# Attention with a local window and global keys, then a SoLU layer: other token runs, sums spread by TensorE in the first batch, constant matmuls and a new order

## The chip, the core and the metric

The kernel runs on one core of a Trainium2 chip. The core has five engines, each with its own row of instructions that it takes strictly in order: TensorE (PE; its weight loads are listed as PEld), VectorE (DVE), ScalarE (ACT), GpSimd (POOL) and SyncE (SP). Transfers between DRAM and the on-chip memory (SBUF) are issued by SP, ACT or POOL and run on 16 DMA engines that all of them share. TensorE writes into PSUM, eight banks of 128 partitions by 2 KB; DVE and ACT read it there. The metric is the device time of one execution in microseconds; less is better.

## What is computed

Four batches, eight heads, 768 tokens, 64 columns a head. A query sees the 8 first keys of its sequence (global) and the 96 keys up to itself (local), with a bias that falls linearly with distance, by a slope for each head. The result, heads side by side, is the 3072 x 512 input x of a feed-forward layer.

```python
scores = scale * np.matmul(q, k.transpose(0, 1, 3, 2))
keep = is_global | is_local
scores = np.where(keep, scores - slopes[:, None, None] * dist, -1e9)
a = np.exp(scores - max); a = a / sum(a)
x = np.matmul(a, v)                       # to 3072 x 512
h = x @ w_in                              # 512 x 1024
solu = h * softmax(h)
ln = (solu - mean) / sqrt(var + 1e-6) * g_ln
out = ln @ w_out                          # 1024 x 512
```

## The kernel before, in words

Everything is written as *steps*: an engine, an estimated duration, a priority, the steps it depends on, the buffers it takes and frees, and a function that emits its instructions. `Plan.order` plays the steps through with these estimates, at each free engine the waiting step of the lowest priority number first, and the functions are then called in that order. The order is therefore fixed before the run: the priorities come from the table `PRIO`, one number for each step, and on the chip each engine waits at the head of its row until that instruction's operands are there. A late operand holds up everything behind it on that engine.

Heads go in pairs: head 2p on partitions 0 to 63, head 2p+1 on 64 to 127. For each batch:

- *Loads.* k and q of a pair come with `load_heads`, eight tokens of 64 columns a head on one partition (`JW` = 8), so 96 partitions hold the 768 tokens and each piece of a transfer has 2,048 bytes. In batch 0 the first 256 tokens come apart in natural order (`load_first`, tiles `knat`, `qnat`), the other 512 in runs of eight on 64 partitions. v comes in blocks of 128 tokens (`load_v`), its first and last 64 tokens for the odd heads with `load_ends` (tile `vt`), the eight global rows with `load_globals` (tile `vgn`).
- *Cast and transposition.* POOL casts to 16 bit (L698, L694), TensorE transposes through PSUM (L714), DVE copies to `kT` (L733) and `qT` (L729). `kT` is put back in token order by that copy; `qT` is left as [8, 96], token 8g + j at [j, g], and so all that has queries as columns has them as eight pieces with a stride, up to the product at the end.
- *Scores.* Blocks of 64 keys against the up to 160 queries that can see them. A bias matmul (L822, from the table `bw`) and a score matmul (L840), both in 64 x 64 blocks of the array, fill a pair of banks; ACT takes the exponential to `eb` (L848). The global keys of all heads are scored at once (L883, then `eg`, L894). Batch 0 has three such groups, of 256 queries each, the other batches two.
- *Sums.* A *unit* is 256 queries (batch 0) or 384. TensorE adds up the exponentials of all heads with blocks of ones (L905, L912), ACT takes a logarithm (L920) and the exponential of its negative (L923), which is the reciprocal. SP stores it to DRAM (`rd`, L553) and loads it back to all 64 partitions of each head (`rb`, L559).
- *Products.* For two pairs at a time TensorE multiplies the exponentials by v (L992) and the global ones by `vgz` (L979) in two half-steps, between which DVE reads one element (`tick`, L1002). DVE multiplies by `rb` and puts the tokens back in order: `xT` (L1019).

For each of the 24 tiles of 128 tokens: the wide projection (L1051, eight matmuls of 512 columns), ACT's exponential (L1058), DVE's product with h (`uu`, L1061), ACT's squares (L1065), eight transposes (L1072) copied by DVE to `uT` (L1076), the output projection (L1110, eight matmuls of 512 columns), ACT's scaling to `osb` (L1116) and SP's store. `w_out` is scaled by g on DVE (L625), its mean over rows is taken by eight matmuls (L631) and subtracted (L635); the output projection needs that.

The lines that set the order around the change:

```python
    def release(self, owner, what, deps):
        self.step("Q", 0, 0, deps, None, free=[(owner, what)])
...
    if PRIO:
        for s, pr in zip(plan.steps, PRIO.split()):
            s["prio"] = int(pr)
    for s in plan.order():
        if s["fn"] is not None:
            s["fn"]()
```

## Time and profile before

| | us |
|---|---|
| median of 3 runs | 222.46 |
| lowest and highest | 219.66, 223.21 |
| the profiled execution: its time | 223.18 |
| the profiled execution: its span, first to last instruction | 221.5 |
| busy in that span: PE, DVE, ACT, POOL | 174.9, 112.6, 112.9, 65.0 |

The profile shows one execution. The page divides the span into 40 equal slices and gives for each the busy share of an engine in tenths. Its list of groups puts together the instructions of one line, operation and shape, with their count, busy time and mean duration. The order of time lists instructions with start, duration and, in brackets, how long the engine was idle before and what ended that. Matmuls overlap, so what a row of them costs is read from start to start. All moved 35.23 MB by DMA.

### The profile page before, as it was taken

Reading aid. Unit: us, or ns where it says so; the run is one execution under the profiler, and the core shown is the slowest. Engines: PE = TensorE matmul, PEld = TensorE weight load, DVE = VectorE, ACT = ScalarE, POOL = GpSimd, SP = SyncE. Lnnn points to the kernel's source line nnn. Section 1 sums busy time; section 2 is a strip of 40 time slices with the busy share of each in tenths; the row PEclk is TensorE's granted clock in tenths of the full one; section 3 lists DMA queues with packets and bytes.
Section 4 is the critical chain, followed back from the end, with each engine's and each line's share of the span. In section 5 each row is a group of like instructions: output and inputs, shape, how many; then the busy total and the mean of one; then the engine's idle time right before and its main releaser. Section 6 shows DMA issues by size and latency. Waiting matters only on the chain. (4 is left out here: it accounts for less than half of the span.)

```text
span 221.5 us, 6271 instructions
## 1 busy us (share of the span) xinstructions
PE 174.9 (79%) x2636; PEld 103.2 (47%) x2636; DVE 112.6 (51%) x238; ACT 112.9 (51%) x202; POOL 65.0 (29%) x140
## 2 busy tenths in 40 slices
PE   0036837677988979997879989779997999998890
PEld 0014416555664646564544546455555455434440
DVE  0465367223574554865534656352772368484540
ACT  2003302432682367693455888364785674566752
POOL 7854187430392166433072008300100000000000
PEclk9999995555999999999988999999999999999998
DMA  6999999994299992999995039631603156300222
GB/s 178 252 202 304 189 206 206 235 259 91 66 259 253 291 222 69 238 251 269 248 231 132 18 113 225 146 145 50 145 0 147 22 130 143 142 3 0 95 95 96
DMA packets 47387, 35.23 MB, mean 159 GB/s; under 512 B 32440, under 2 KB 37120, under 8 KB 47360
## 3 DMA queue, kind: packets, MB, share of 16 engines
q1 hardware_dynamic: 44560, 33.24, 61.1%
q0 software_dynamic: 544, 1.05, 2.9%
q10 hardware_dynamic: 2256, 0.56, 1.1%
q8 instruction: 20, 0.33, 0.7%
q14 instruction: 7, 0.06, 0.1%
HBM read 29.50 MB, written 6.39 MB: 162 GB/s over the span
## 5 line engine op out<-in xcount | busy, mean ns | idle before, releaser
L848 ACT ACTIVATE eb<-bank 128x960 f16<-128x960 f32 (+3 forms) x36 | 29.9, 856 | 48.2 <-PE bank L840 47.7
L1051 PE MATMUL bank<-w_in_sb,xT 128*128 128x512 f16 x192 | 47.1, 389 | 0.1
L1110 PE MATMUL bank<-gw_out_sb,uT 128*128 128x512 f16 x192 | 44.8, 379 | 1.0 <-DVE xT L1019 0.4
L1061 DVE SCALAR_TENSOR_TENSOR uu<-ef,bank 128x1024 f16<-128x1024 f16 x24 | 29.2, 1216 | 12.5 <-ACT ef L1058 12.4
L1058 ACT ACTIVATE ef<-bank 128x1024 f16<-128x1024 f32 x24 | 24.5, 1020 | 16.3 <-PE bank L1051 16.2
L1019 DVE TENSOR_TENSOR xT<-bank,rb 128x384 f16<-128x384 f32 (+1 forms) x36 | 25.2, 730 | 10.1 <-PE bank L992 5.0
L1110 PEld LDWEIGHTS <-uT 128*128 128x128 f16 x192 | 17.8, 97 | 21.3 <-DVE uT L1076 1.4
L1051 PEld LDWEIGHTS <-xT 128*128 128x128 f16 x192 | 17.9, 99 | 20.3 <-issue 1.9
L1065 ACT ACTIVATE sq<-uu 128x1024 f16<-128x1024 f16 x24 | 25.2, 1051 | 3.9 <-DVE uu L1061 3.7
L714 PE MATMUL bank<-ident,k 96*128 96x96 f16 (+2 forms) x136 | 10.2, 220 | 19.5 <-POOL k L694 10.9
L733 DVE COPY kT<-bank 128x768 f16<-128x768 f16 (+2 forms) x20 | 15.4, 769 | 19.4 <-PE bank L714 16.8
L992 PE MATMUL bank<-eb,v 64*64 64x160 f16 (+4 forms) x464 | 20.5, 230 | 4.1 <-DVE tick L1002 1.3
L1076 DVE COPY uT<-bank 128x1024 f16<-128x1024 f16 x24 | 16.4, 689 | 14.1 <-PE bank L1072 6.1
L698 POOL CAST k<-k 96x1024 f16<-96x1024 f32 (+1 forms) x16 | 16.5, 1035 | 23.1 <-PE bank L714 11.3
L698 POOL CAST q<-q 96x1024 f16<-96x1024 f32 (+1 forms) x16 | 16.4, 1036 | 19.9 <-PE bank L714 13.3
L1116 ACT ACTIVATE osb<-bank,rstd 128x512 f32<-128x512 f32 x24 | 15.9, 684 | 11.2 <-PE bank L1110 5.3
L714 PEld LDWEIGHTS <-k 96*128 96x128 f16 (+2 forms) x136 | 7.9, 106 | 23.6 <-POOL k L694 11.1
L992 PEld LDWEIGHTS <-v 64*64 64x64 f16 x464 | 11.8, 107 | 12.1 <-issue 8.1
L822 PE MATMUL bank<-bw,identb 64*64 64x160 f16 (+4 forms) x448 | 16.0, 251 | 0.8 <-DVE uu L1061 0.6
L783 POOL CAST v<-v 128x704 f16<-128x704 f32 (+2 forms) x24 | 13.4, 576 | 10.7 <-DMA v<-in_v_dram 10.0
L840 PE MATMUL bank<-qT,kT 64*64 64x160 f16 (+4 forms) x416 | 15.6, 250 | 0.5 <-DVE qT L729 0.5
L1072 PE MATMUL bank<-ident,uu 128*128 128x128 f16 x192 | 14.4, 219 | 1.8 <-DVE uT L1076 0.9
(82 smaller groups left out, 176.3 us busy)
## 6 DMA issues: line engine op xcount, KB each, us to landing
out_dram<-osb SPq DMA_DIRECT2D x24, 256.0 KB
q<-in_q_dram SPq DMA_DIRECT2D x12, 384.0 KB
k<-in_k_dram SPq DMA_DIRECT2D x12, 384.0 KB
rb<-rd SPq DMA_DIRECT2D x12, 384.0 KB
v<-in_v_dram SPq DMA_DIRECT2D x12, 192.0 KB
w_out<-in_moe_w_out_dram SPq DMA_DIRECT2D x4, 512.0 KB
v<-in_v_dram SPq DMA_DIRECT2D x12, 160.0 KB
rb<-rd SPq DMA_DIRECT2D x6, 256.0 KB
```

Of the source, the lines that this page charges most:

```text
L698: nc.gpsimd.tensor_copy(out=o[0:w], in_=a[0:w].rearrange("p h j d -> p j h d"))
L714: nc.tensor.transpose(out=pt[:, j * m : j * m + m], in_=src[0:m, j].rearrange("p h d -> p (h d)"), identity=ident[0:m, 0:m])
L822: nc.tensor.matmul(out=sc[o : o + 64, par, col : col + n * JW], lhsT=identb[r, r], rhs=v3(bw[r, p])[:, :, a : a + n], start=(par, h) not i ...
L848: ex["fn"] = (lambda ex=ex, qk=qk, gw=gw: nc.scalar.activation(out=eb[at(qk, "eb")][:, :, 0:gw], in_=big(qk)[:, :, 0:gw], func=AF.Exp, sca ...
L992: nc.tensor.matmul(out=o_[64 * h : 64 * h + 64, :, gl : gl + m], lhsT=vv[r, v_at(vi, h, c), d0 + d, :], rhs=view(eb[at(e_own[b, gi, d0 + d ...
L1019: nc.vector.tensor_tensor(out=xT[at(xt_own[b], "xT")][:, p, q0:q1].rearrange("p (g j) -> p g j", j=JW), in0=one(av, d)[:, 0:w].rearrange(" ...
L1051: nc.tensor.matmul(out=ph()[:, ts(fh, 512)], lhsT=xT[at(xt_own[b], "xT")][:, j, ts(t % NA, P)], rhs=w_in_sb[:, j, ts(fh, 512)], start=(j = ...
L1058: ex["fn"] = lambda g1=g1, t=t, ph=ph: nc.scalar.activation(out=ef[at(g1, "ef")], in_=ph(), func=AF.Exp, accum_out=s0[:, t : t + 1])
L1061: u["fn"] = lambda u=u, g1=g1, t=t, ph=ph: nc.vector.scalar_tensor_tensor(out=uu[at(u, "uu")], in0=ef[at(g1, "ef")], scalar=USC, in1=ph(), ...
L1065: sqs["fn"] = lambda u=u, t=t: nc.scalar.activation(out=sq, in_=uu[at(u, "uu")], func=AF.Square, accum_out=s2[:, t : t + 1])
L1076: el["fn"] = lambda lt=lt, el=el: nc.vector.tensor_copy(out=uT[at(el, "uT")].rearrange("p c f -> p (c f)"), in_=one(lt).bitcast(FP16))
L1110: nc.tensor.matmul(out=one(g2), lhsT=uT[at(el_x, "uT")][:, c, :], rhs=gw_out_sb[:, c, :], start=(c == 0), stop=(c == NFC - 1))
```

## The change

It does these things at once.

- *Runs of six.* `load_heads` puts six tokens on each of 128 partitions (pieces of 1,536 bytes); batch 0's rest comes in runs of four (1,024 bytes). Casts are 768 and 512 columns wide on 128 partitions, a pair takes six (four) 128 x 128 transposes instead of eight, and DVE's copy puts both `kT` and `qT` in token order. With that all query columns are contiguous everywhere: scores, `eb`, sums, the products with v and `xT`.
- *Global products.* The product with `vgz` is written as one 64 x 64 block for each head instead of 64 x 128 for two.
- *Sums spread by TensorE in batch 0* (`DIRECT`, three units). No sum step, no store and load of `rd` and `rb`: each pair gets its own two half-steps, in which every matmul with v has a twin with ones (`onesv`, `onesz`), so that the sums come out on all 64 partitions of the head in a second bank. ACT takes logarithm and exponential of it for each pair and DVE multiplies.
- *w_out's first scaling* goes from DVE to ACT. `load_ends` becomes two loads for each batch, eight in all. `uT` has seven buffers instead of four.
- *Constant matmuls.* Where the plan sees TensorE idle by over 330 ns between 3 and 60 us of its own time, before that step it issues matmuls of a constant tile `busy16` (128 x 512) into a bank that is free, for 80% of that gap at 216 ns each: 63 in all, 29 of them ahead of the first transpose, 34 at 13 places up to before the second half of batch 0's products.
- *A new order*: other estimates, at most four large loads under way in the plan (`LDQ`), and another table `PRIO`.

```diff
+    WARM = (3000, 60000)
...
+                    spot = min((i for i in range(8) if banks[i] or i in mine),
+                               key=lambda i: bank_at[i], default=None)
+                    if e == "PE" and now < self.WARM[1] and s["dur"] and spot is not None:
+                        idle = now - max(busy[e], bank_at[spot] + 100, self.WARM[0])
+                        if idle > 330:
+                            s["warm"] = (spot, int(idle * 0.8 / 216))
...
     for s in plan.order():
+        spot, count = s["warm"]
+        for _ in range(count):
+            nc.tensor.matmul(out=bank[spot // 2][:, spot % 2, :], lhsT=busy16[:, 0:P],
+                             rhs=busy16, start=True, stop=True)
...
-    def load_heads(src, dst, b, p, lo, hi):
+    def load_heads(src, dst, b, p, lo, run):
         rows = src[b, 2 * p]
-        n = hi - lo
         nc.sync.dma_start(
-            out=dst[0:n].rearrange("g h j d -> g h (j d)"),
-            in_=bass.AP(tensor=rows.tensor, offset=rows.offset + lo * JW * D,
-                        ap=[[JW * D, n], [S * D, 2], [1, JW * D]]))
+            out=dst[:, 0 : 2 * run * D].rearrange("g (h x) -> g h x", h=2),
+            in_=bass.AP(tensor=rows.tensor, offset=rows.offset + lo * D,
+                        ap=[[run * D, P], [S * D, 2], [1, run * D]]))
...
-            wr.append(step("DVE", 484, 16000 + 100 * j, [w_out_st[j // 2], g_st] + bias_st + [far_st], lambda j=j:
-                           nc.vector.tensor_scalar(
-                               out=gw_out_sb[:, j, :], in0=w_out32[:, j, :],
-                               scalar1=g32[:, j : j + 1], scalar2=None, op0=ALU.mult)))
+            wr.append(step("ACT", 640, 16000 + 100 * j,
+                           [w_out_st[j // 2], g_st] + bias_st + [far_st], lambda j=j:
+                           nc.scalar.activation(
+                               out=gw_out_sb[:, j, :], in_=w_out32[:, j, :], func=AF.Copy,
+                               scale=g32[:, j : j + 1])))
...
-                    for j in range(n):
-                        nc.tensor.transpose(out=pt[:, j * m : j * m + m],
-                                            in_=src[0:m, j].rearrange("p h d -> p (h d)"),
-                                            identity=ident[0:m, 0:m])
+                    for j in range(run):
+                        nc.tensor.transpose(out=pt[:, j * P : j * P + P], in_=src[:, j, :],
+                                            identity=ident)
...
+    DIRECT = {(0, 0), (0, 1), (0, 2)}
...
+            for ti_, duo in enumerate([(p, None) for p in range(NPR)] if direct else
+                                      [(p, p + 1) for p in range(0, NPR, 2)]):
...
                             nc.tensor.matmul(
-                                out=o_[64 * h : 64 * h + 64, :, gl : gl + m],
-                                lhsT=vv[r, v_at(vi, h, c), d0 + d, :],
+                                out=o_[64 * h : 64 * h + 64, gl : gl + m],
+                                lhsT=onesv[r, :] if pv is None else vv[r, v_at(vi, h, c), pair, :],
...
+                if direct:
+                    ln = step("ACT", 110 + w, ta + 1000, [aw, table_st], None, take="lns",
+                              free=[(av, 1)])
+                    re = step("ACT", 140 + w, ta + 1500, [ln], None, take="rr",
+                              free=[(ln, "lns")])
```

Of the order three places matter for what follows. Names are tiles with a running number; the line numbers of the changed program are its own.

SP, the loads around the middle of the load stage. Before, the first k and q of batch 1 (96 partitions) stand among batch 0's v, the v ends and the `rb` of batch 0's first unit:

```order
L498 DMA k_0_92<-in_k_dram 96x2x512
L518 DMA vt_81<-in_v_dram 64x16x64
L498 DMA q_1_96<-in_q_dram 96x2x512
L559 DMA rb_143<-rd_141 64x4x256 x2
L511 DMA v_0_104<-in_v_dram 128x4x64
L498 DMA k_1_93<-in_k_dram 96x2x512
L511 DMA v_1_105<-in_v_dram 128x4x64
```

These are its rows 27 to 33; all of `w_out` (rows 1, 5 and 11) has been asked for long before. Now, rows 46 to 50:

```order
L518 DMA k_0_95<-in_k_dram 128x2x384
L518 DMA q_0_98<-in_q_dram 128x2x384
L644 DMA w_out_70<-in_moe_w_out_dram 128x2x512
L518 DMA k_1_96<-in_k_dram 128x2x384
L518 DMA k_2_97<-in_k_dram 128x2x384
```

The k and q loads of batch 1 come behind all of batch 0, and `w_out` has moved from the front to among them, its last part to row 48.

DVE, around the products of a unit of batch 0. Before, the first unit, with one k copy ahead:

```order
L733 COPY kT_113<-bank_160 128x768
L1002 COPY tick<-bank_157 128x1
L1002 COPY tick<-bank_158 128x1
L1019 TENSOR_TENSOR xT_90<-bank_160,rb_143 128x256
L1019 TENSOR_TENSOR xT_90<-bank_158,rb_143 128x256
L1019 TENSOR_TENSOR xT_90<-bank_157,rb_143 128x256
L729 COPY qT_118<-bank_160 128x768
```

Now, the end of the last two units, with the copies of batch 1 (128x768) among the products:

```order
L750 COPY qT_121<-bank_165 128x768
L1028 COPY tick<-bank_163 128x1
L1056 TENSOR_TENSOR xT_93<-bank_164,rr_141 128x256
L1056 TENSOR_TENSOR xT_93<-bank_165,rr_140 128x256
L750 COPY kT_114<-bank_165 128x768
L1056 TENSOR_TENSOR xT_93<-bank_166,rr_140 128x256
L1056 TENSOR_TENSOR xT_93<-bank_166,rr_141 128x256
L663 SCALAR_TENSOR_TENSOR gw_out_sb<-w_out_70,g_72,bank_163 128x512 x5
```

The products take ACT's reciprocals (`rr`) in place of `rb`, a copy of a batch 1 load stands ahead of the last two, and the second scaling of `w_out` has moved behind all of batch 0's products.

ACT, after the first unit's exponentials. Before, one logarithm and one exponential for the unit:

```order
L894 ACTIVATE eg_116<-bank_160,gbias 128x128
L848 ACTIVATE eb_126<-bank_157 128x2x288
L920 ACTIVATE lns_135<-bank_160 128x256
L923 ACTIVATE rr_137<-lns_135 128x256
L848 ACTIVATE eb_127<-bank_157 128x2x320
```

Now, a pair of them for each pair of heads:

```order
L1033 ACTIVATE lns_138<-bank_166 128x256
L1037 ACTIVATE rr_140<-lns_138 128x256
L1033 ACTIVATE lns_139<-bank_164 128x256
L1033 ACTIVATE lns_138<-bank_165 128x256
L1037 ACTIVATE rr_141<-lns_139 128x256
L1033 ACTIVATE lns_139<-bank_163 128x256
```

All score exponentials of batch 0 but four now stand ahead of these. On TensorE (a list that is too long to show) the first two tiles' projections come behind the first unit's products; then, ahead of the third tile, stand the products of units 1 and 2, four transpose sets of batch 1 and the mean over `w_out`, and all scores of batch 1 come behind it. Before, the third tile stood behind the first two tiles' output projections and all scores of batch 1.

More of the change, by code (lines that the diff above doesn't have):

```diff
@@ L21 @@
 WIN = 160
-JW = 8
-BG = BLK // JW
-WG = WIN // JW
+RUN = 6
 USC = 1.0 / 16.0
@@ L686, in do_part, with cast @@
                     need = [dma]
[L687 removed]
+                cs = step("POOL", 394 if natural else 20 + 1.01 * n, t0 - 1200, need, None,
                           take=nm + "16_", free=[(iss, nm + "32_")] if iss else [])
[L690 to L692 removed]
+                def cast(cs=cs, iss=iss, x32=x32, x16=x16, nm=nm, run=run, natural=natural, p=p):
+                    o = x16[at(cs, nm + "16_")][:, 0:run].rearrange("p j (h d) -> p j h d", h=2)
@@ L918 @@
-            sm["fn"] = sums
-            ln = step("ACT", 110 + w, tS + 1000, [sm], None, free=[(sm, "one")])
-            ln["fn"] = lambda sm=sm, w=w: nc.scalar.activation(
-                out=lns[at(sm, "lns")][:, 0:w], in_=one(sm)[:, 0:w], func=AF.Ln)
-            re = step("ACT", 140 + w, tS + 1500, [ln], None, take="rr", free=[(sm, "lns")])
-            re["fn"] = lambda re=re, sm=sm, w=w: nc.scalar.activation(
-                out=rr[at(re, "rr")][:, 0:w], in_=lns[at(sm, "lns")][:, 0:w], func=AF.Exp, scale=-1.0)
@@ L937 @@
[L937 to L946 removed]
+            direct = (b, ui) in DIRECT
@@ new lines @@
+            lastu = ui == len(UNITS[b]) - 1
+            if lastu:
+                plan.release(kg_own[b], "kg", kg_users)
+                for p in range(NPR):
+                    plan.release(own[p, "k"], "kT", qk_of[p])
+                    plan.release(own[p, "q"], "qT", qk_of[p])
+            turn_of = []
+            by = [[x for x in todo if x[2] == par] for par in range(2)]
+            turns = [[(i, d) for i in range(max(map(len, by))) for d in (0, 1)
+                      if i < len(by[ph ^ d])] for ph in range(2)]
@@ new lines, in pe @@
+                        pv = duo[d]
+                        pair = duo[0] if pv is None else pv
+                        o_ = one(av, d)[:, 0:w]
+                        for h in range(2):
+                            x = h ^ par
+                            r = slice(64 * x, 64 * x + 64)
+                            if i < 0:
+                                nc.tensor.matmul(
+                                    out=o_[64 * h : 64 * h + 64, x * n : x * n + n],
+                                    lhsT=(onesz[r, 2 * pair + h] if pv is None else
+                                          vgz[r, b, 2 * pair + h, :]),
+                                    rhs=eg[at(gs, "eg")][r, 0:hw_],
+                                    start=False, stop=False,
+                                    tile_position=(64 * x, 64 * h), skip_group_check=True)
+                                continue
+                            gi, c, _, col, nn, lo, gl, m = by[par][i]
+                            nc.tensor.matmul(
+                                out=o_[64 * h : 64 * h + 64, gl : gl + m],
+                                lhsT=onesv[r, :] if pv is None else vv[r, v_at(vi, h, c), pair, :],
+                                rhs=view(eb[at(e_own[b, gi, pair], "eb")], r, par, col, nn,
@@ L1094, in stats @@
                 nc.vector.tensor_tensor(out=a, in0=a, in1=c, op=ALU.add)
-            st = step("DVE", 850, tt + 5700, [chain[x][1] for x in grp], stats)
+            st = step("DVE", 700, tt + 5700, [chain[x][1] for x in grp], stats)
             def rs(lo=lo, hi=hi):
```

391 lines of the change are left out of this document (195 added, 196 removed), and 170 rows, old and new, of the table PRIO.

## The prediction

> **What bounds the kernel now.** I read the page first, then the busy time by stage, then the order of time around the points where the stages change. The page's slices are 5.54 us each:
>
> ```profile
> span 221.5 us, 6271 instructions
> ...
> PE   0036837677988979997879989779997999998890
> ...
> PEclk9999995555999999999988999999999999999998
> DMA  6999999994299992999995039631603156300222
> GB/s 178 252 202 304 189 206 206 235 259 91 66 259 253 291 222 69 238 251 269 248 231 132 18 113 225 146 145 50 145 0 147 22 130 143 142 3 0 95 95 96
> ```
>
> Two regimes: up to slice 9 (50 us) the DMA row is full and TensorE is half idle; from slice 11 on TensorE is at 7 to 9 tenths to the end. The same by stage (length; busy us of PE, PEld, DVE, ACT, POOL, each with its count; granted clock, DMA share, GB/s):
>
> ```profile
> 32.50:56.70 24.20, 17.61 (x418) 13.38 (x417) 10.44 (x20) 8.35 (x14) 9.07 (x12) 0.51 0.88 188
> 56.70:79.45 22.75, 19.98 (x391) 13.08 (x384) 13.63 (x29) 12.15 (x22) 11.00 (x21) 1.00 0.97 233
> 79.45:216.90 137.45, 124.79 (x1674) 69.75 (x1673) 74.55 (x149) 86.89 (x160) 25.56 (x36) 0.99 0.49 128
> ```
>
> After 79.45 us TensorE is the bound: 124.79 us busy, 12.66 idle. The two cuts are where the first tokens reach the wide projection (L1051), and where the third tile does:
>
> ```profile
> 9.92 0.40 PE L714 MATMUL bank<-ident,k 128*128 128x128 f16 x2 [9.92 <-POOL k L694]
> ...
> 23.58 0.65 ACT L848 ACTIVATE eb<-bank 128x576 f16<-128x576 f32 x1 [0.27 <-PE bank L840]
> ...
> 25.58 3.57 PE L631 MATMUL bank<-gw_out_sb,onesm 128*128 128x512 f16 x8 [0.47 <-ACT lns L920]
> ...
> 34.16 1.64 SPq L559 DMA_DIRECT2D rb<-rd  x2
> ...
> 46.53 0.35 PE L992 MATMUL bank<-eb,v 64*64 64x160 f16 x4 [0.33 <-DVE kT L733]
> 46.81 0.29 PE L979 MATMUL bank<-eg,vgz 64*128 64x128 f16 x2
> 47.03 0.32 PE L992 MATMUL bank<-eb,v 64*64 64x128 f16 x4
> 47.27 0.64 PE L883 MATMUL bank<-qT,kg 128*64 128x128 f16 x8
> ...
> 56.73 1.90 PE L1051 MATMUL bank<-w_in_sb,xT 128*128 128x512 f16 x8
> ...
> 60.53 0.84 PE L714 MATMUL bank<-ident,k 96*128 96x96 f16 x16
> ...
> 61.31 0.40 PE L822 MATMUL bank<-bw,identb 64*64 64x160 f16 x12
> ...
> 61.54 0.38 PE L840 MATMUL bank<-qT,kT 64*64 64x160 f16 x12
> ...
> 61.85 0.62 PE L1072 MATMUL bank<-ident,uu 128*128 128x128 f16 x8
> ...
> 79.45 0.81 PE L1051 MATMUL bank<-w_in_sb,xT 128*128 128x512 f16 x3
> ...
> 114.39 3.53 PE L1051 MATMUL bank<-w_in_sb,xT 128*128 128x512 f16 x8
> ```
>
> and from the chain that ended last (start, us, what), a piece of the end:
>
> ```profile
> 181.17 1.73 PE bank L1110 x8
> ```
>
> Unit 0 (the first 256 queries) has its exponentials at 24.23 us, its first products with v (L992) only at 46.53, its first projection at 56.73. The reciprocals were asked for at 34.16, so the round trip through DRAM is not what held it; TensorE's own row of work and the loads were. Eight 512-column matmuls take 1.73 us at 181.17 and 3.57 at 25.58: half speed, although the clock row says 9 there. So that row does not show the early clock; the durations do. Half speed again in slices 6 to 9, and at 114.39 (3.53 us for what takes 1.90 at 56.73).
>
> **The change, part by part.** Let A be the start of the third tile's projection, 79.45 now. All before A is the load stage, all behind it TensorE's row.
>
> *When the loads let A start.* In the new order the last load that A stands behind is SP's 49th, a k pair of batch 1: its transposes and copy stand ahead of the last two unit 2 products, and the mean over w_out stands ahead of A on TensorE. Adding up the issue list, SP has then asked for 8.36 MB, ACT for 0.56, POOL for w_in (1.05 MB as stored): 9.97 MB. The GB/s row gives 9.81 MB by 44.3 us and 9.97 by 44.9. Behind it come a cast, six transposes, a copy, a product and the mean. Their prices and those of the parts below:
>
> ```profile
> L1065 ACT ACTIVATE sq<-uu 128x1024 f16<-128x1024 f16 x24 | 25.2, 1051 | 3.9 <-DVE uu L1061 3.7
> L1058 ACT ACTIVATE ef<-bank 128x1024 f16<-128x1024 f32 x24 | 24.5, 1020 | 16.3 <-PE bank L1051 16.2
> L1019 DVE TENSOR_TENSOR xT<-bank,rb 128x384 f16<-128x384 f32 x24 | 18.3, 797 | 6.8 <-PE bank L992 3.6 <-PE bank L912 1.5 <-PE bank L1110 1.0
> ...
> L1116 ACT ACTIVATE osb<-bank,rstd 128x512 f32<-128x512 f32 x24 | 15.9, 684 | 11.2 <-PE bank L1110 5.3 <-PE bank L992 2.8 <-PE bank L1072 0.8
> ...
> L698 POOL CAST k<-k 96x1024 f16<-96x1024 f32 x12 | 12.4, 1036 | 20.3 <-PE bank L714 11.3 <-DMA k<-in_k_dram 8.5 <-POOL q L698 0.5
> ...
> L733 DVE COPY kT<-bank 128x768 f16<-128x768 f16 x12 | 11.5, 955 | 16.2 <-PE bank L714 13.7 <-ACT osb L1116 2.6
> ...
> L729 DVE COPY qT<-bank 128x768 f16<-128x768 f16 x12 | 6.6, 554 | 5.5 <-PE bank L714 2.8 <-PE bank L1110 1.5 <-PE bank L992 0.8
> ...
> L635 DVE SCALAR_TENSOR_TENSOR gw_out_sb<-w_out,g,bank 128x512 f16<-128x512 f32 x8 | 5.9, 743 | 6.4 <-PE bank L631 5.0 <-PE bank L714 1.4
> ...
> L923 ACT ACTIVATE rr<-lns 128x256 f32<-128x256 f32 x3 | 1.2, 416 | 0.1
> ...
> L920 ACT ACTIVATE lns<-bank 128x256 f32<-128x256 f32 x3 | 1.1, 383 | 1.5 <-PE bank L912 0.9 <-DVE xT L1019 0.6
> ```
>
> The cast falls from 1024 to 768 columns: between 1.04 (no gain) and 0.78 (by columns); I take 0.78. Transposes 0.39 (60.53 to 61.31 holds two sets), copy 0.96, product about 0.4 (557 x 256/384, below), mean 1.73: 4.26 us, A at 49.2 by the loads.
>
> *When TensorE lets A start.* Unit 0: exponentials at 24.23, then eight half-steps of ten matmuls, 0.74 us each at half speed (46.53 to 47.27), 0.37 at full: 3.0; a logarithm and an exponential 0.80, a product 0.4, and a us for the steps ordered in between: first projection at about 29.5. From it to A stand two projections 3.46, two score groups 1.08 (0.54 each, 61.31 to 61.85), two sets of tile transposes at the like 1.08, 28 transposes 1.4, 304 half-step matmuls (a pair now has its own two half-steps, with ones beside v, and no separate sum step) at 0.037 = 11.2, the mean 1.73: 20 us, so A at 49.5. ACT has there two exp and square pairs (4.1), eight ln/exp pairs (6.4), the scaling of w_out, new on it (8 at the 0.68 of osb, the nearest 512-column row, 5.5), and four score exponentials (2.6): 18.6 of 20 us. Loads, TensorE and ACT nearly coincide, and each waits for the others, so I add 2.5 us, an estimate: **A at 52**. Range: 46 (the better case below) to 69.5 (all of TensorE's 20 us at half speed).
>
> *What is left behind A.* Now: 79.45 to 221.5, 142.05 us. At A the new order has not yet done two output projections (3.46), five transpose sets (1.95), the eight score groups of batch 1 (8 x 0.54 = 4.32) and its two global score steps (half of 0.64 each, the row at 47.27 being at half speed): +10.4. It loses the half-speed stretch at 114.39 if no gap goes before it: -1.6 (kept: 0). The v products write whole rows instead of eight strided pieces:
>
> ```profile
> 101.53 0.26 PE L979 MATMUL bank<-eg,vgz 64*128 64x192 f16 x2
> 101.72 0.38 PE L992 MATMUL bank<-eb,v 64*64 64x160 f16 x12
> 102.03 0.26 PE L979 MATMUL bank<-eg,vgz 64*128 64x192 f16 x2
> ```
>
> Twelve take 0.31 us, 26 ns each, where twelve score matmuls whose output was always whole take 0.23 (61.31 to 61.54), 19 ns. Over 336 of them that is at most 2.4 us, at least 0: -1.2. The global pair becomes four 64x64 blocks: now 0.19 for two; four at 26 to 50 ns are 0.10 to 0.20, 24 times: -2.2 to +0.2, I take -1.2. Sum behind A: 142.05 + 10.4 - 1.6 - 2.4 = 148.4 us.
>
> *Costed at nothing, with the cover.* The 12 q copies of batches 1 to 3 grow from 554 to 955 at most (the k row, which now has the same form), +4.8 us; the 24 products fall from 797 to 557 at best (743 x 384/512), -5.8. DVE is busy 74 of 137 us behind A, which covers either sign. POOL sheds about 6 us of casts and was at 26 of 137. Of the 63 constant matmuls 29 stand ahead of the first transpose, where TensorE was idle to 9.92 us anyway: 12.9 us if all at half speed (3.57/8 each), 8.2 if the clock rises after eight; the others lie where a wait is planned, 34 x 0.22 to 34 x 0.45 us (7 to 15) if the wait is not there, nothing if it is; I take nothing, since the row has 2.5 us of waits in the sum before A and half speed is a rival of its own. Behind such a filler stands the next real step, and DVE's copies or ACT's exponentials wait for that. Batch 0's three DRAM round trips (1.6 MB) go: a product now waits for ACT's exponential, and behind it, in DVE's row, stand the k and q copies and the later products; meanwhile the pair holds two PSUM banks. Six more v-end loads, and batch 1 to 3's global v, now stand ahead of most k loads on SP; their bytes are in the 8.36 MB. The identity is built later in POOL's row, behind a v cast that waits for two loads: the first transpose may come after 9.92 us, covered by the k and q loads as far as those are late too. Seven uT buffers let transposes run ahead and take nothing away.
>
> Sum: 52 + 148.4 = 200.4 span. The profiled execution's time, 223.18, is 1.68 above its span, so **202 us**, against 222.46 for the median (the profiled one is 0.3% above it).
>
> **Two rules weighed.** Stages again, columns as above:
>
> ```profile
> 35.90:42.20 6.30, 6.20 (x174) 5.20 (x174) 3.80 (x8) 3.75 (x6) 3.91 (x7) 0.50 1.17 210
> ...
> 52.80:56.30 3.50, 3.10 (x86) 2.37 (x87) 2.24 (x4) 1.95 (x5) 0.00 (x0) 0.50 0.03 7
> 56.30:60.00 3.70, 3.70 (x50) 2.04 (x39) 0.95 (x3) 2.58 (x5) 0.91 (x1) 0.98 0.15 23
> ```
>
> The clock rose near 56.3 us after 3.5 us that were 3.1 us busy, and did not rise in 6.3 us that were 6.2 busy, from 35.9. The Trainium skill (TensorE: Matmul & The Clock Gate, Part 1: The HAM clock gate) says a busy window of about 3.4 us frees the clock and an idle one halves it; its Part 4 says transposes do not count as busy. By the first the constant matmuls carry the clock and A stays at 52; by the second, with early work rich in transposes, A moves towards 69.5, which is the rival on the half clock. The trace speaks against the first at 35.9 to 42.2 and for it at 56.3; transposes stood in both stretches, so it does not decide the second.
> The Trainium skill (DMA: Bandwidth & Descriptors, Why small descriptors are slow) gives each packet about three beats on top of one per 32 bytes: pieces of 1,536 or 1,024 bytes for 2,048 would cost 2 to 5% of those loads, under 1 us in the sum. No row here prices a packet by size.
>
> **Rivals.**
> - *Half clock before A.* Busy TensorE does not lift the clock, as from 35.9 to 42.2, or the gaps that remain let it fall. For: slices 6 to 9. Against: 63 fillers in the gaps. With half of the 20 us slow A is 60, the time 210; with all of it 69.5, the time 220.
> - *Loads bound by packets.* Each k or q load goes from 192 pieces to 256 (batch 0's rest from 128 to 256): 2,048 more up to batch 2's end, 512 in batch 3. At 235 GB/s (the common full slice) a 2,048-byte piece takes 139 ns of one of 16 engines; if each costs this whatever its size, that is 17.8 and 4.4 us. Batch 1's first projection (114.39 now) stands behind 21.3 MB, 90.6 us at 235 GB/s; with 17.8 and the 4.3 of the chain it starts at 112.7, and the 107.1 us behind it, 4.4 and 1.7 end at 226, on the wrong side; past 227 from 146 ns a piece. Against: slices of 291 and 304 GB/s, by which a piece takes 108 ns and the end is 221.
> - *The front does not move.* One late POOL cast or ACT step, each in a fixed order, holds all: A at 64 to 73, 214 to 223. For: three engines are near full before A.
> - *Better.* With the half-steps at the score matmuls' pace (19 against 37 ns) and loads at 250 GB/s both bounds of A come to 44; A at 46, and idle behind it from 12.7 to 7: 190.
>
> **How the numbers follow.** My case, A from 48 with some idle saved to 58, is 196 to 208: 0.50. Partly cold, 208 to 214: 0.16. Fully cold or front held, 214 to 223: 0.14. Better, below 196: 0.12. Packets, 209 to above 226: 0.08. The range 190 to 215 leaves out 0.2 or less. About 2% can be told from no change here: faster than 218 is 0.84 (my case, partly cold, better, some of the rest), within 2% is 0.12, slower 0.04 (half of the packets' case).
>
> **What would show it.** Right: L1089's third tile near 52 us, 512-column matmuls at 0.215 us from about 10 us on, TensorE idle under 13 us behind A. Wrong: early fillers spaced 0.43 us; DMA full until 100 us with POOL casts waiting on k loads; ACT full with TensorE waiting on it before A.

## The result, and the profile after

The changed kernel takes **210.72 us** (median of 4 runs, 210.17 to 211.83) against 221.98 us (4 runs, 219.66 to 223.21) for the kernel before, measured beside it: a ratio of 0.953, 95% interval 0.944 to 0.962. It is faster, by about half of what was forecast (202 us, range 190 to 215). The profiled execution took 211.01 us, its span is 209.3. In some executions a kernel takes over 1.5% longer than in its fastest: the ratios leave these out, as does the second time column of the table below, and the profiles of e3_later, e4_before_fill and e10_none are of such executions.

The page of the changed kernel (slices of 5.23 us):

```profile
span 209.3 us, 6581 instructions
...
PE   7949777787699989678499899989988988999961
...
PEclk9976999969979999999969999999999999999997
DMA  5999678981959799579909955110731861110213
GB/s 117 267 224 239 131 198 231 297 285 32 317 162 280 227 272 274 152 178 226 302 20 237 212 118 147 55 50 5 204 105 56 203 153 50 53 50 0 100 70 131
```

TensorE's first seven slices, which were 0 to 8, are 4 to 9, but part of that are the constant matmuls. The DMA row is no longer full before A: slice 9, 47 to 52 us, moved 32 GB/s.

By stage, cut at the first projection, at A (the start of the third tile's projection) and at TensorE's last matmul (length; busy us of PE, PEld, DVE, ACT, POOL with counts; granted clock, DMA share, GB/s):

```profile
0.00:34.67 34.67, 25.62 (x428) 14.20 (x428) 15.13 (x44) 10.69 (x20) 23.06 (x85) 0.90 0.84 193
34.67:60.68 26.01, 20.70 (x393) 12.23 (x390) 12.37 (x31) 17.13 (x38) 9.79 (x20) 0.87 0.74 227
60.68:204.90 144.22, 130.68 (x1964) 76.10 (x1962) 81.70 (x162) 94.06 (x168) 24.15 (x39) 0.99 0.53 142
```

A stands at 60.68 us; forecast were 52. Behind A lie 209.3 - 60.68 = 148.6 us; forecast were 148.4. So the whole error is ahead of A. What TensorE did there (start, us, line, what; in brackets the idle time ahead and what ended it):

```profile
1.52 8.52 PE L1166 MATMUL bank<-busy 128*128 128x512 f16 x29 [1.52 <-DVE busy L597]
...
28.36 0.40 PE L738 MATMUL bank<-ident,k 128*128 128x128 f16 x4
29.93 1.02 PE L1166 MATMUL bank<-busy 128*128 128x512 f16 x4 [1.18 <-DVE xT L1056]
30.79 0.39 PE L738 MATMUL bank<-ident,q 128*128 128x128 f16 x4
31.02 0.59 PE L1166 MATMUL bank<-busy 128*128 128x512 f16 x2
32.29 0.38 PE L738 MATMUL bank<-ident,q 128*128 128x128 f16 x4 [0.68 <-DVE qT L750]
...
43.56 1.01 PE L1166 MATMUL bank<-busy 128*128 128x512 f16 x2 [0.93 <-DVE uT L1114]
44.50 0.50 PE L839 MATMUL bank<-bw,identb 64*64 64x32 f16 x12
...
57.55 3.30 PE L659 MATMUL bank<-gw_out_sb,onesm 128*128 128x512 f16 x8
60.68 3.62 PE L1089 MATMUL bank<-w_in_sb,xT 128*128 128x512 f16 x16
```

The 29 opening constant matmuls (L1166) lie ahead of the first transpose at 11.14 us and are free. The later 34 are not: a group waits for a PSUM bank that DVE still reads (at 29.93 for a product), then it runs, and only then comes the transpose that makes progress. The chain that ended at A, by line:

```profile
by line: PE bank L1166 14.4%; PE bank L738 11.4%; DVE kT L750 6.6%; issue 6.5%; PE bank L1089 5.9%; PE bank L1018 5.8%; DVE qT L750 5.4%; PE bank L659 5.1%; DVE xT L1056 4.2%; PE bank L839 4.2%; PE bank L857 2.9%; DVE uu L1099 2.0%; DVE uT 
```

The constant matmuls lead it with 14.4% of 60.68 us, 8.7 us. That A is late by as much (60.68 for 52) is partly chance: the matmuls also raise the clock for the work behind them. Whether they cost that or earn it back by the clock is the first question for the experiments.

### The profile page after: what moved, and what is told of

The parts are those of the page before. It is cut to its first block, busy times and chain, and to the rows that moved or that the text cites. A ratio compares the mean times of both kernels' runs of the same rounds, so it can differ in the third digit from the quotient of the medians.

```text
span 209.3 us, 6581 instructions
## 1 busy us (share of the span) xinstructions
PE 177.0 (85%) x2779; PEld 102.5 (49%) x2779; DVE 109.2 (52%) x237; ACT 123.1 (59%) x228; POOL 57.0 (27%) x142
## 3 DMA queue, kind: packets, MB, share of 16 engines
q1 hardware_dynamic: 45536, 31.64, 55.4%
## 4 chain that ended last, share of the span: by engine, by line
PE 63%; DVE 16%; ACT 8%; issue 6%; POOL 5%; ACTq 0%; DVEq 0%; POOLq 0%
PE bank L1148 20%; PE bank L1089 15%; PE bank L738 6%; PE bank L1166 4%; PE bank L1018 4%; PE bank L1110 4%; DVE qT L750 3%; PE bank L839 3%; DVE kT L750 3%; DVE xT L1056 3%; DVE uT L1114 2%; DVE uu L1099 2%; ACT osb L1154 2%; PE bank L857 2%; ACT sq L1103 2%
## 5 line engine op out<-in xcount | busy, mean ns | idle before, releaser
L1089 PE MATMUL bank<-w_in_sb,xT 128*128 128x512 f16 x192 | 44.9, 380 | 0.3
L1099 DVE SCALAR_TENSOR_TENSOR uu<-ef,bank 128x1024 f16<-128x1024 f16 x24 | 29.2, 1217 | 11.9 <-ACT ef L1096 11.8
L1089 PEld LDWEIGHTS <-xT 128*128 128x128 f16 x192 | 18.2, 98 | 20.6 <-issue 0.9
L1166 PE MATMUL bank<-busy 128*128 128x512 f16 x63 | 20.0, 454 | 7.5 <-DVE xT L1056 2.7
L750 DVE COPY qT<-bank 128x768 f16<-128x768 f16 (+1 forms) x16 | 14.2, 888 | 12.3 <-PE bank L738 7.2
L1018 PE MATMUL bank<-eb,v 64*64 64x160 f16 (+4 forms) x464 | 17.2, 222 | 2.5 <-DVE tick L1028 1.2
L1056 DVE TENSOR_TENSOR xT<-bank,rb 128x384 f16<-128x384 f32 x24 | 12.3, 551 | 12.2 <-PE bank L1148 4.2
L725 POOL CAST q<-q 128x768 f16<-128x768 f32 (+1 forms) x16 | 12.4, 773 | 22.9 <-PE bank L738 17.1
L725 POOL CAST k<-k 128x768 f16<-128x768 f32 (+1 forms) x16 | 12.3, 774 | 21.0 <-PE bank L738 16.3
L750 DVE COPY kT<-bank 128x768 f16<-128x768 f16 (+1 forms) x16 | 14.1, 888 | 6.3 <-PE bank L738 5.3
L1018 PEld LDWEIGHTS <-v 64*64 64x64 f16 x464 | 13.4, 108 | 6.4 <-issue 6.1
L839 PEld LDWEIGHTS <-identb 64*64 64x64 f16 x448 | 9.9, 113 | 11.2 <-issue 10.2
```

The lines of the kernel that those rows point to most:

```text
L725: nc.gpsimd.tensor_copy(out=o, in_=a)
L750: nc.vector.tensor_copy(out=d_.rearrange("p (g j) -> p g j", j=run), in_=pt.rearrange("p (j g) -> p g j", j=run))
L839: nc.tensor.matmul(out=sc[o : o + 64, par, col : col + n], lhsT=identb[r, r], rhs=bw[r, p, a : a + n], start=(par, h) not in seen, stop=False,
L1018: nc.tensor.matmul(out=o_[64 * h : 64 * h + 64, gl : gl + m], lhsT=onesv[r, :] if pv is None else vv[r, v_at(vi, h, c), pair, :], rhs=view ...
L1089: nc.tensor.matmul(out=ph()[:, ts(fh, 512)], lhsT=xT[at(xt_own[b], "xT")][:, j, ts(t % NA, P)], rhs=w_in_sb[:, j, ts(fh, 512)], start=(j = ...
L1099: u["fn"] = lambda u=u, g1=g1, t=t, ph=ph: nc.vector.scalar_tensor_tensor(out=uu[at(u, "uu")], in0=ef[at(g1, "ef")], scalar=USC, in1=ph(), ...
```

## The experiments

Times are medians: of all executions, and of those that the ratio uses. Each ratio is against the kernel before, run on the same chip. The text goes by the second time.

| run | constant matmuls | time us, all | time us, of the ratio | ratio (95%) | first projection | A | span |
|---|---|---|---|---|---|---|---|
| the change | 63 | 210.72 | 210.72 (4) | 0.953 (0.944 to 0.962) | 34.67 | 60.68 | 209.3 |
| e1_none | 0 | 205.28 | 205.14 (3) | 0.930 (0.918 to 0.942) | 32.65 | 53.23 | 201.3 |
| e10_none (the same kernel) | 0 | 205.68 | 205.12 (4) | 0.925 (0.918 to 0.931) | 33.97 | 57.91 | 208.8 |
| e2_opening | 29 | 205.18 | 205.18 (4) | 0.932 (0.922 to 0.942) | 31.54 | 55.01 | 204.6 |
| e3_later | 34 | 210.19 | 207.73 (2) | 0.944 (0.928 to 0.960) | 35.62 | 62.28 | 210.5 |
| e9_short | 63, 64 columns | 210.89 | 210.89 (4) | 0.953 (0.947 to 0.959) | 35.64 | 59.83 | 208.9 |
| e12_own | 63, own bank | 208.09 | 207.60 (3) | 0.940 (0.928 to 0.951) | 34.06 | 57.23 | 205.9 |
| e6_pieces | 0 | 209.53 | 209.28 (3) | 0.947 (0.939 to 0.956) | 34.92 | 59.58 | 207.6 |
| e7_scale_dve | 0 | 210.08 | 208.45 (2) | 0.948 (0.941 to 0.956) | 32.64 | 57.30 | 205.5 |
| e8_tail | 0 | 202.85 | 202.85 (6) | 0.924 (0.920 to 0.929) | 33.84 | 55.12 | 202.9 |
| e11_tail (the same kernel) | 0 | 202.72 | 202.72 (6) | 0.916 (0.911 to 0.920) | 34.01 | 54.90 | 200.4 |
| e4_before_fill (kernel before) | 73 | 218.54 | 217.28 (6) | 0.988 (0.982 to 0.993) | 55.14 | 79.25 | 217.5 |

In brackets is the number of executions. The last three columns are of one profiled execution each. That A is of a single execution matters: the same kernel gave 53.23 and 57.91, the second with the eight matmuls of the mean at half speed. Up to A e8_tail and e11_tail are this kernel too, and gave 55.12 and 54.90.

```profile
54.84 3.28 PE L659 MATMUL bank<-gw_out_sb,onesm 128*128 128x512 f16 x8
57.91 3.96 PE L1089 MATMUL bank<-w_in_sb,xT 128*128 128x512 f16 x16
```

So a difference in A of less than some 5 us is only believed where the medians go with it.

### The constant matmuls: none, the opening ones, the later ones

```diff
 e1_none
-        for _ in range(count):
+        for _ in range(0):
 e2_opening (e3_later: count if opened else 0)
+        opened = opened or s["start"] > 12000
-        for _ in range(count):
+        for _ in range(0 if opened else count):
```

> The changed kernel with none of its 63 constant matmuls; every other instruction stands in the same row on every engine. Theory P (they stand on the path): 14.4% of the chain of waits ahead of the third tile's wide projection (A, 60.68 us) is these matmuls, 8.7 us; without them A comes near 52 and the time is near 202. Theory C (they earn their time by the clock): the other TensorE work of that chain is 35%, 21 us; at half clock it grows by up to 15, A comes near 67 and the time near 217. If both hold and cancel, 208 to 213.

> The changed kernel with the 29 constant matmuls ahead of the first transpose and none of the 34 later ones. These 29 end at 10.04 us, before the first transpose at 11.14, so they are off the path. P: as with none or a little better, A near 52, time near 202. C: the clock falls without the later ones, A 62 to 67, time 212 to 217.

> The changed kernel with the 34 later constant matmuls and none of the 29 opening ones. P and C both: the opening ones cost nothing; if the clock at 12 to 20 us was their doing, A comes 1 to 2 us later (62, time 212); if not (the clock was down at 12 to 20 us with them), nothing changes: 210 to 211.

Without any, 205.14 us: 5.6 us less, and the ratio's interval (0.918 to 0.931 in e10_none) lies clear of the changed kernel's (0.944 to 0.962). The stages of e1_none:

```profile
0.00:32.65 32.65, 15.41 (x381) 12.05 (x382) 15.11 (x44) 10.77 (x20) 22.77 (x84) 1.00 0.89 204
32.65:53.23 20.58, 15.23 (x376) 10.90 (x374) 12.28 (x31) 17.22 (x39) 8.74 (x19) 0.92 0.89 278
53.23:196.94 143.71, 130.75 (x1964) 76.43 (x1962) 81.75 (x163) 93.94 (x168) 25.52 (x41) 0.99 0.53 144
```

A falls to 53.23, and the same 143.7 us of TensorE's row follow as in the changed kernel (144.2). Theory P holds for the sum: the price of the constant matmuls is paid ahead of A and goes into the end. The opening 29 change nothing that can be measured in the time (205.18 against 205.14). So the loss is with the later 34: it comes when they are put behind the opening ones. Alone (e3_later) they give 207.73 of two executions, with an interval (0.928 to 0.960) that overlaps both sides, so how much of the loss they bring without the opening ones is open. Theory C had forecast 217 for none; as a sum it falls, but part of it is there, as the next section shows.

### Is it their run time, their wait, or both

```diff
 e9_short
-            nc.tensor.matmul(out=bank[spot // 2][:, spot % 2, :], lhsT=busy16[:, 0:P],
-                             rhs=busy16, start=True, stop=True)
+            nc.tensor.matmul(out=bank[spot // 2][:, spot % 2, 0:64], lhsT=busy16[:, 0:P],
+                             rhs=busy16[:, 0:64], start=True, stop=True)
 e12_own
+        own = [2 * i if t == "big" else i for t, i in s["slot"] if t in ("big", "one")]
+        spot = own[0] if own else spot
```

> The changed kernel with all 63 constant matmuls in their places and with their waits, but of 64 columns for 512: an eighth of the run time. If it is their run time on the path that costs (8.7 us ahead of A in the chain), an eighth of it is left: A 53.5 to 55, time 204 to 206, as without them. If it is that they wait for a PSUM bank ahead of the real step, whatever their length, A stays at 58 to 61, time 209 to 211.

> The changed kernel with all 63 constant matmuls at full length, each group writing the PSUM bank of the step that follows it in place of the bank that the plan saw free for longest: a group then waits for nothing that the step itself would not wait for. If the foreign bank's wait is what costs (a score group at 44.5 us stood behind fillers that waited 0.93 us for a uT copy, a transpose behind fillers that waited 1.18 us for a product), A falls from 60.7 to 54 to 57 and the time to 204 to 207. If it is the place in the row and the run time itself, A stays at 59 to 61, time 209 to 211.

An eighth of the length saves nothing: 210.89 us. That does not clear the run time, since two things change with the length. Two places in e9_short show them:

```profile
31.07 0.28 PE L1166 MATMUL bank<-busy 128*128 128x64 f16 x4 [1.18 <-DVE xT L1056]
31.19 0.39 PE L738 MATMUL bank<-ident,q 128*128 128x128 f16 x4
31.41 0.22 PE L1166 MATMUL bank<-busy 128*128 128x64 f16 x2
32.69 0.55 PE L738 MATMUL bank<-ident,q 128*128 128x128 f16 x4 [1.06 <-DVE qT L750]
33.17 0.50 PE L839 MATMUL bank<-bw,identb 64*64 64x32 f16 x12
...
44.57 0.27 PE L1166 MATMUL bank<-busy 128*128 128x64 f16 x2 [0.78 <-DVE uT L1114]
44.76 0.50 PE L839 MATMUL bank<-bw,identb 64*64 64x32 f16 x12
```

The waits are all still there. At 44.57 a score group stands behind two fillers that wait 0.78 us for a uT copy to leave a bank. In e1_none that score group has no wait at all (40.24, straight behind eight transposes). The short ones also leave the clock low: the twelve bias matmuls at 33.17 take 0.50 us, in the changed kernel 0.34 (32.61).

With the group in the bank of its own successor (e12_own), the foreign waits go, and the score group follows at once and at full speed:

```profile
28.90 1.02 PE L1168 MATMUL bank<-busy 128*128 128x512 f16 x4 [0.85 <-DVE kT L750]
...
41.86 0.59 PE L1168 MATMUL bank<-busy 128*128 128x512 f16 x2
42.38 0.34 PE L839 MATMUL bank<-bw,identb 64*64 64x32 f16 x12
```

A is 57.23, the time 207.60, just outside both expectations. What was paid for what can be read by adding up TensorE's time from the first transpose to A. The second row of each pair is that of the constant matmuls alone, and idle is the length less the busy time. The changed kernel:

```profile
11.14:60.68 49.54, 37.81 (x787) 23.07 (x787) 21.25 (x54) 26.54 (x57) 23.77 (x52) 0.86 0.80 212
11.14:60.68 49.54, 11.49 (x34) 3.51 (x34) 0.86 0.80 212
```

e1_none, then e9_short and e12_own:

```profile
11.14:53.23 42.09, 30.63 (x754) 22.85 (x754) 21.15 (x54) 26.71 (x57) 22.43 (x50) 0.96 0.91 244
...
11.14:59.83 48.69, 36.76 (x788) 27.88 (x788) 21.35 (x54) 26.89 (x57) 22.54 (x50) 0.86 0.78 209
11.14:59.83 48.69, 3.69 (x34) 2.77 (x34) 0.86 0.78 209
...
11.14:57.23 46.09, 36.21 (x787) 22.47 (x787) 21.25 (x54) 26.55 (x57) 23.86 (x52) 0.89 0.85 228
11.14:57.23 46.09, 10.63 (x34) 3.39 (x34) 0.89 0.85 228
```

| run | A | constant matmuls, us | other TensorE work, us | idle, us |
|---|---|---|---|---|
| none: e1_none, e11_tail, e8_tail, e10_none | 53.2, 54.9, 55.1, 57.9 | 0 | 30.6, 32.8, 32.9, 34.5 | 11.5, 10.9, 11.1, 12.2 |
| the change | 60.7 | 11.5 | 26.3 | 11.7 |
| e9_short | 59.8 | 3.7 | 33.1 | 11.9 |
| e12_own | 57.2 | 10.6 | 25.6 | 9.9 |

So both theories are at work. The later fillers took none of the idle time away: TensorE idles 11.7 us with them and 10.9 to 12.2 without, because a group waits for its bank about as long as the next step would have waited, and only then runs. Their 11.5 us of run time are therefore added to the row. The clock pays part of this back: the other work takes 26.3 us for 30.6 to 34.5. The short fillers add little, but the idle time stays and the other work takes 33.1 us, so they lose what the long ones earn. The own bank takes some 2 us of waits out. In the medians 3.1 of the 5.6 us come back with it (210.72 to 207.60) and 2.5 stay; the intervals overlap, so these two numbers are good to a microsecond or two. Each row of the table is one execution, and a filler's busy time overlaps with its neighbours by some tenths. Short ones in the own bank weren't tried.

### The same fillers in the kernel before

The rule of the changed planner, put into the planner of the kernel before: 36 constant matmuls ahead of its first q transposes and, by the count in the trace, 37 later (73; the expectation has 71); no step moves.

> The kernel before, in its own order, with 71 constant matmuls in the gaps of its own plan by the same rule (36 ahead of its first q transposes, 35 later). P: the 35 later ones push its third projection (79.45 us) back by 35 x 0.22 to 35 x 0.45, 8 to 16 us, or by about half of that if half of them meet a real wait: 226 to 238. C: TensorE was at half clock from 32 to 56 us and 15.5 of 24 us busy there; at full clock that gives up to 8 us back: 214. Cancelling: 220 to 224.

Ratio 0.988 (0.982 to 0.993): some 1% faster, between the theories. The fillers push nothing back there: A is at 79.25 us, 79.45 without them. What this execution gains over the profiled one of before lies behind A, where no filler stands (217.5 - 79.25 = 138.2 us for 142.05):

```profile
79.25 1.89 PE L1066 MATMUL bank<-w_in_sb,xT 128*128 128x512 f16 x8
...
82.96 1.24 PE L1066 MATMUL bank<-w_in_sb,xT 128*128 128x512 f16 x5
```

The fourth tile starts at 82.96 (84.43 in the profile of before, where TensorE pauses for 1.37 us at 83.18, ended by "issue"), and in this execution batch 1's first projection takes 1.90 us instead of 3.53. Whether the fillers have to do with either, these runs don't show. Why they cost nothing ahead of A can be seen in part: 49 of the 73 stand between 10 and 32 us, where TensorE's idle time falls from 9.6 to 3.3 us, and only seven behind 32 us. There they do fill idle time, which the 34 of the changed kernel do not.

### Parts of the change that carry the gain

Batch 0's reciprocals by DRAM again (e5_round), in place of TensorE's sums:

```diff
-    DIRECT = {(0, 0), (0, 1), (0, 2)}
+    DIRECT = set()
```

The steps that this brings back have priorities of their own, all others keep theirs; no constant matmuls.

> Without constant matmuls, and batch 0's reciprocals through DRAM again as in the kernel before (sums for the four pairs, store, two spreads, product by the spread tile), for all three of its units. TensorE's row up to the first projection is otherwise that of the run without constant matmuls; behind the third tile the planner's order comes out worse, so the time is not compared, only the first projection (32.65 us without constant matmuls) and A (53.23). Theory D (the sums on TensorE bring the first projection forward): a store and two spreads of 384 KB with their issues are 5 to 8 us, first projection 38 to 41, A 58 to 64. Theory O (the new order and the loads bring it): 33 to 35, A 53 to 56.

```profile
38.30 3.39 PE L1100 MATMUL bank<-w_in_sb,xT 128*128 128x512 f16 x8 [5.04 <-DVE xT L1060]
```

The first projection comes at 38.30 for 32.65 us, and TensorE has stood 5.04 us waiting for the product. For the first projection theory D holds at its lower end: the sums on TensorE are worth 5.65 us of the 24 by which it moved (56.73 to 32.65), or 4.3 to 4.5 against e8_tail, e10_none and e11_tail (33.84 to 34.01). A came at 76.72, far outside both theories (58 to 64, 53 to 56). It and the time of this one execution, 243.02, are put down to the worse order behind the first tiles and say nothing of the round trip; whether the other 18 us are the order or the loads is not separated by any run here.

Pieces of half the size, by two issues for each k or q load (e6_pieces):

```diff
-        nc.sync.dma_start(
-            out=dst[:, 0 : 2 * run * D].rearrange("g (h x) -> g h x", h=2),
+        hw = run // 2 * D
+        for a in range(2):
+            nc.sync.dma_start(
+                out=dst[:, 0 : 2 * run * D].rearrange("g (h a x) -> g a h x", h=2, a=2)[:, a],
```

> Without constant matmuls, each k or q load of runs in two DMAs of half-runs: the same bytes to the same places in twice as many pieces (768 or 512 bytes for 1,536 or 1,024), 8,192 more in all, and 32 more issues on SP of 0.4 us. Rival of packets (a piece costs 139 ns of one of 16 engines whatever its size): 4,096 more pieces ahead of A are 36 us of DMA time, A past 80, time over 235. By bytes: the DMA side does not change, SP's issues are mostly covered by its waits: A 53 to 56, time 205 to 209. Between, by the price it has.

209.28 us, 4 more than without: just above the range by bytes, far from the rival of packets. The page's queue rows (packets, MB, share of 16 engines) of e6_pieces,

```profile
span 207.6 us, 6512 instructions
...
q1 hardware_dynamic: 54240, 31.64, 57.7%
```

and of e1_none:

```profile
span 201.3 us, 6455 instructions
...
q1 hardware_dynamic: 45536, 31.64, 56.8%
```

The same bytes took 0.577 x 207.6 x 16 = 1,917 engine-us for 1,829: 87 us for 8,704 pieces more, 10 ns a piece (7.6 against e10_none, 0.554 x 208.8 x 16 = 1,851). All ten profiled executions with these 45,536 packets lie between 1,829 and 1,876, so a piece more costs 5 to 10 ns. Spread over 16 engines, 87 us are 5.4 in the whole span, half of it behind A, where the DMA row has room: at most 2.7 us (an estimate) of the 4. What is also delayed is SP's row, which in e1_none issues with hardly a pause from 16 to 36 us, at 0.4 to 0.65 us each. Its first k load of batch 1 there,

```profile
30.09 0.55 SPq L518 DMA_DIRECT2D k<-in_k_dram  x1
```

and in e6_pieces:

```profile
33.19 2.06 SPq L520 DMA_DIRECT2D k<-in_k_dram  x2
```

Three microseconds late: SP's issues are a resource of their own in this stage. How much of the 4 us they make, and how much the pieces, is not separated. Nor does TensorE show it as a longer wait: from 11.14 us to A it idles 11.5 us, as without the split, and its work takes 37.0 us for 30.6 to 34.5 at a granted clock of 0.82 for 0.90 to 0.96.

The first scaling of `w_out` on DVE, as before, at the same place in the program (e7_scale_dve):

```diff
-                           nc.scalar.activation(
-                               out=gw_out_sb[:, j, :], in_=w_out32[:, j, :], func=AF.Copy,
-                               scale=g32[:, j : j + 1])))
+                           nc.vector.tensor_scalar(
+                               out=gw_out_sb[:, j, :], in0=w_out32[:, j, :],
+                               scalar1=g32[:, j : j + 1], scalar2=None, op0=ALU.mult)))
```

> Without constant matmuls, and the eight scalings of w_out on DVE as before (8 x 0.48) in place of ACT (8 x 0.69), at the same place in the program. If ACT's row sets A (it was 5.84 of 8 us busy from 40 to 48): A earlier by up to 2 us, time 203 to 205. If DVE's row sets it: later by up to 3.9 us, 206 to 209. If neither, 205.

```profile
54.28 3.19 PE L659 MATMUL bank<-gw_out_sb,onesm 128*128 128x512 f16 x8
57.30 3.62 PE L1089 MATMUL bank<-w_in_sb,xT 128*128 128x512 f16 x16
```

208.45 us (two executions), 3.3 more than the two runs without it, as forecast if DVE's row sets A; ACT's has room. How it does so is only partly seen. From the first projection to A a wait of 1.0 us for a product of DVE is new, but that stretch is 4.1 us longer than in e1_none (24.66 for 20.58), and 3.1 of these are busy time of TensorE at a lower clock (0.79 for 0.92); the mean alone, at half speed (3.19 for 1.89), is 1.3. A at 57.30 lies within what the kernel without this edit gave (53.2 to 57.9).

### A version that beats both

In e1_none the last output projections each wait for the copy of the one before, since all three write one PSUM bank while others are free:

```profile
189.65 1.90 PE L1148 MATMUL bank<-gw_out_sb,uT 128*128 128x512 f16 x8
192.33 1.89 PE L1148 MATMUL bank<-gw_out_sb,uT 128*128 128x512 f16 x8 [0.78 <-ACT osb L1154]
```

```diff
+    seq = plan.order()
+    ends = [s for s in seq if s.get("cls") == 1][-3:]
+    ends[1]["slot"] = [("one", 0)]
+    ends[2]["slot"] = [("one", 2)]
```

> Without constant matmuls, and the last three output projections write three PSUM banks instead of one. In the run without constant matmuls the last two each waited for the copy of the one before (0.78 and 0.82 us): 1.6 us less, span near 199.7 for 201.3, time near 203.7, ratio to before 0.922. If the copies or the stores are the end's bound: no change.

> The kernel without constant matmuls once more, beside the next one on the same chip: 204 to 206.

> The kernel without constant matmuls and with three PSUM banks for the last three output projections, beside the run above: the two waits of 0.78 and 0.82 us gone, 1.6 us below it (202.5 to 204.5). If the earlier difference (205.28 to 202.85) was the chip's spread, no difference.

The three now run as one piece (e11_tail):

```profile
191.35 5.35 PE L1148 MATMUL bank<-gw_out_sb,uT 128*128 128x512 f16 x24
```

202.85 and 202.72 us, ratios 0.924 (0.920 to 0.929) and 0.916 (0.911 to 0.920). Beside its twin on the same chip it is 2.4 us faster (205.12 to 202.72); 1.6 are the two waits, the rest is within the spread. So the change without its constant matmuls, and with these two lines, is 7 to 8 us faster than the change as made.

## Why the prediction was right, and where it was off

- *The direction and the two regimes.* Right: the load stage shrank, TensorE's row behind A stayed the bound.
- *The time.* 202 us was forecast, 210.72 came, inside the range of 190 to 215 but outside "my case" (196 to 208, 0.50). It fell where "partly cold" (208 to 214) had been put, and for another reason, so that the range held it is partly luck.
- *What is left behind A: 148.4 us.* Right: 148.6, and 148.0 to 149.6 in the seven profiled executions of e1, e2, e3, e6, e7, e9 and e12 (span less A in the table; 150.9 in e10_none). Two of its terms, the v products and the global ones, were too small together, and for another reason than the one given. The starts of the single matmuls behind A, taken from the traces, show that v matmuls follow each other no faster now (13.8 ns, mean of 297) than with the strided pieces (14.2 ns, mean of 294). What fell is the step from a v matmul to a global one and back: 0.16 and 0.18 us in the median while the global one was 64x128 among 64x64, 0.04 and 0.05 us now. In the changed kernel:

```profile
99.23 0.28 PE L1009 MATMUL bank<-eg,vgz 64*64 64x192 f16 x4
99.31 0.38 PE L1018 MATMUL bank<-eb,v 64*64 64x160 f16 x12
99.50 0.27 PE L1009 MATMUL bank<-eg,vgz 64*64 64x192 f16 x4
```

  All intervals between v and global matmuls add up to 12.6 us before and 7.2 now: 5.4 us saved for the 2.4 forecast. That the sum came out all the same means that some 3 us were spent that are not in it; a pause of 2.7 us at 100.8 us is the largest piece seen, the rest was not worked out.
- *A at 52 us.* The step that failed is the one on the constant matmuls: "the others lie where a wait is planned, 34 x 0.22 to 34 x 0.45 us (7 to 15) if the wait is not there, nothing if it is; I take nothing". They measured 8.7 us in the chain and 5.6 us in the time. The waits were there (TensorE idles 11.5 us from its first transpose to A without fillers), and yet the cost was not nothing, for the fillers did not run inside them: a filler needs a PSUM bank and waits for that bank's last reader, so the idle time stayed (11.7 us) and 11.5 us of run time came on top, of which the clock gave back 4 to 8. Without the fillers A came at 53.2 to 55.1 in three executions, 57.9 in a fourth, and the time at 205.1: the rest of the sum was 3 us too low.
- *The bounds of A.* The first projection came at 32.65 (no fillers), not 29.5, and the stretch to A took 20.6 us, not 22.5; the two nearly cancel. I had counted the twelve extra small loads (six v ends, batch 1 to 3's global v) by their bytes; on SP they are issues of 0.6 us in a row that is full from 16 to 36 us. What they cost was not tried by itself.
- *The half clock before A* (0.16 in my chances). Partly there: the mean at 3.30 us in the changed kernel, the score group at 44.50 at half speed. It is not what set the fillers' loss: the other work ahead of A was quicker with them (26.3 us) than without (30.6 to 34.5). In the kernel without fillers it is there, and is worth at least these 4 to 8 us of TensorE's work.
- *Loads bound by packets* (0.08). Out: 5 to 10 ns of an engine for a piece more, not 139.
- *The front does not move.* Out: A moved by 18.8 us with the fillers and 21.5 to 26.2 without. Its mechanism, one step late in an in-order row, may be what costs e7_scale_dve 3.3 us.
- *Better.* Not reached by the change, nor by the version that beats it (202.7).
- *What would show it.* None of the three signs of being right quite came: the third tile at 60.68 us and not near 52; 512-column matmuls not at 0.215 us from 10 us on (one takes 0.63 at 13.56, and the granted clock is 0.58 from 12 to 20 us); idle behind A up to the last matmul not under 13 us but 144.22 - 130.68 = 13.5. Of the signs of being wrong, the early fillers were spaced 0.29 us on average (29 in 8.52), not 0.43.

## What to carry to other kernels

A matmul that only keeps TensorE busy is work in an in-order row: it needs a PSUM bank, it waits for that bank's last reader, and what stands behind it waits too. If it waits as long as the next step would have, it fills no idle time and its run time is added; the clock gives only part of it back. So compare the idle time with and without it. Put such fillers only where the chain of waits shows an idle time that no tuning of buffers will take away, here the first 10 us (where they cost nothing and brought nothing either), and look there for what they bring before adding any elsewhere. And take the last steps of a kernel from a profile: two waits for one bank, with others free, were 0.8% of the whole.

## What the hardware showed that was not expected

- *The clock went down within 3.5 us behind 8.5 us of load.* In the changed kernel the 29 opening matmuls end at 10.04 us; up to 13.5 TensorE only transposes, with gaps of 0.7 to 1.1 us, and then a single constant matmul takes 0.63 us:

```profile
13.39 0.37 PE L738 MATMUL bank<-ident,q 128*128 128x128 f16 x2 [0.78 <-DVE kT L750]
13.56 0.63 PE L1166 MATMUL bank<-busy 128*128 128x512 f16 x1
```

  The granted clock is 0.58 from 12 to 16 us and 0.57 from 16 to 20. The Trainium skill (TensorE: Matmul & The Clock Gate, Part 1) has one idle window of about 3.4 us halve the clock, and its Part 4 does not count transposes as busy; 10.04 to 13.5 agrees with the first, and does not decide the second, since TensorE was busy for only 0.9 us of that stretch, all of it transposes. The burst did carry the first transposes (0.38 us for four at 11.14; 0.59 in e1_none), but not the time: e2_opening is as fast as e1_none.
- *A change of block shape costs TensorE time.* Going from 64x64 blocks to a 64x128 one and back took 0.16 and 0.18 us in the kernel before, 0.04 and 0.05 us where all are 64x64; the stride of the output rows cost nothing (14.2 and 13.8 ns a matmul).
- *A DMA piece costs little.* 5 to 10 ns of an engine for each more, at 512 to 768 bytes. The Trainium skill (DMA: Bandwidth & Descriptors, Why small descriptors are slow) gives about three beats of overhead a packet, one beat being 32 bytes. At the 139 ns that the forecast worked out for 2,048 bytes, three beats are an estimated 6 ns, the same order.
- *One kernel, two clocks.* The mean took 1.89 us in one execution and 3.28 in another of the same kernel, and A moved by 4.7 us; 3.9 of these are TensorE's work ahead of A taking longer (30.6 and 34.5 us), 0.8 its idle time.
- *TensorE pauses that nothing explains.* In the changed kernel it stops for 2.7 us inside a score group at 100.8 us (ended by "issue"), while the DMA engines are full; in other runs pauses of 1.0 to 3.8 us stand between 92 and 105 us, and the kernel before has 1.37 us at 83.2. Not tried; open.
